# Logarithm and exponential from one activation table, the first stripe masked on VectorE by factor and triangle, stripe 1's products on the whole array, and another order of the written-out list

## The chip, the cores and the metric

The kernel runs on one core of a Trainium2 chip. The metric is the device time in microseconds (us). Before the change it is 226.11 us, the median of three runs (225.96 to 226.34). The profiled execution from which all durations below come took 225.86 us, of which 224.1 us are the span between its first and its last instruction.

## The reference

Two layers follow each other. The first is an attention without softmax whose weights decay with distance; it is written in blocks of 64 rows, with a state that is carried from block to block. The second is a two-layer perceptron on its output.

```python
# q, k, v: 4 batches x 8 heads x 768 rows x 64; lam: one number per head, 0.97 to 0.99
Dmask = np.where(rel >= 0, lam[:, None, None] ** rel[None, :, :], 0.0)
for b in range(nb):
    intra = np.einsum('bhic,bhjc->bhij', qb, kb) * Dmask[None]
    intra = np.einsum('bhij,bhjd->bhid', intra, vb)
    inter = np.einsum('bhid,bhde->bhie', qb * lam_pow[None], kv_state)
    out[:, :, sl] = intra + inter
    kv_state = lam_block * kv_state + np.einsum('bhsd,bhse->bhde', kb * rev_pow, vb)
...
h = x @ w_in                                  # 3072 x 512 by 512 x 2048
g = np.where(h >= 1, h, np.where(h <= -1, 0, (h + 1) ** 2 / 4))
return g @ w_out                              # 2048 x 512
```

## The kernel before

The 3072 rows are cut into eight stripes (`STRIPES`): stripe 0 has four blocks of 128 rows, stripe 1 two, the six others three each. Stripes 0 and 1 together are the first batch. A stripe's eight heads are worked in four pairs. The kernel works in blocks of 128 rows and not of 64, so the decay factors are taken for 128.

The decay is made once, at the start: `ln_lam` is the logarithm of `lam` (line 191, ScalarE), `ex` its product with positions (line 194, VectorE), `dec` the exponential (line 197, ScalarE). Logarithm and exponential come from two activation tables, and each is loaded by an ACT_TABLE_LOAD. `k` and `q` are multiplied by their factors while they are cast to bf16 (`att_cast`). The product of `k` and `q` then lacks one factor per head and the causal triangle: `mask`, built for a pair by two ScalarE instructions (`build_mask`, line 216), holds their product for each head, and one VectorE instruction per pair (`att_mask`, line 371) multiplies the scores by it.

What is done is not scheduled by a program. It is the string `ORDER`, a list of words in the order in which their instructions are recorded. Each engine, and each queue of transfers, executes its own part of the list in that order, and waits for what an instruction needs. A word has a letter, a stripe and a pair, and for casts an engine (a ScalarE, d VectorE, g GpSimd):

- `L01k` loads k of stripe 0, pair 1 (SyncE's queue); in stripes 1 to 3 one load covers two pairs, so `L10v` brings v of stripe 1 for the pairs 0 and 1. In stripe 0 a load of k or v is two transfers, one of q is a single one. `W0` to `W3` load quarters of `w_in`, `W4` to `W7` of `w_out`, on GpSimd's queue with a cast from f32 to bf16 (lines 232 and 236). `L10v@W2` means that this load waits until the one named has landed.
- `k`, `q`, `v` cast; `T`, `Q` transpose k and q on TensorE (line 334) and `t`, `u` copy the transposes out on ScalarE (lines 342, 344); `S` the scores (lines 358, 362), `s` the mask; `R` the new part of the state (lines 416, 422), `r` the state's update on VectorE (lines 435, 444); `O` the output of a pair (lines 472 to 504) and `o` its copy on ScalarE (lines 514, 516).
- `K` is `mlp_in_ko` (line 575): for stripe 0 alone, the part of the first three tiles of `x @ w_in` that needs one pair only. `P03` is one whole tile of `x @ w_in` (four products, line 561), `h03` its relu with bias (line 584, ScalarE), `A00` the rest of the activation for four tiles (lines 541 to 543, VectorE). `Y012` is a quarter of the second product for one block of 128 rows (line 593; the last digit is the quarter of `w_out`), `y` and `U` copy and store the result.
- `D1` and `D2` are one and two products of the identity with itself (line 549) that nobody reads. `B0a` builds a mask, `E` completes the factors of the scan in stripe 0, `J` clears the middle of the v and kz tiles, `G` clears zeros, `z` copies k into a tile with zeros beside it.

`FORMS` has a letter for each stripe, the form of its products. In form p the two heads of a pair use halves of the array: the products of `O` are 128x64 and 64x64 (lines 485 and 504), and the state of a pair is 128x64. In form f both heads use the whole array, with zeros beside the values: v and kz tiles have a zero middle, the state is 128x128 with zeros outside its two corners, the factor with the state is one product per block and not two (lines 472 and 493). In form w, from stripe 4, the transposes are made by DMA.

PSUM has four banks for the perceptron (`pmm`), two for transposes, states and outputs (`pat`), and one tile for the scores (`psp`), so the scores of a pair wait until the mask of the pair before has read them.

Of the kernel before, what the change touches and what calls it, by code (L numbers as in the profile page):

```python
# [8 lines left out]
F32 = mybir.dt.float32  # L9
# [33 lines left out]
v20g y02 T20 T21 Q20 h10 P19 t21 P18 k23d Y002 L21q@W5 v22d Y013 q22g z21a t20 u20 h18 R20 P11  # L43
S20 k22d y01 h19 Q21 P13 h11 P12 u21 L31k q23d P16 L30k z22a Y003 T22 h13 h12 U02 P17 P15 L31q
h16 t22 r20 s20 y00 h17 A10 S21 Q22 k32d s21 P1a u22 Q23 T23 h1a R21 r21 L30q u23 P14 L30v v23g
z23g P1c P1f h15 k33g q30g P1d h14 P1b q31g S22 h1f h1c L31v O20 L40k t23 R23 k31a A11 o20 h1d
s22 P1e Y100 R22 Y110 k30a r23 z31g v32g r22 Y111 S23 O21 h1b L40q h1e Q30 T30 A12 s23 o21 A13
L40v Y101 u30 t30 O22 z30g T31 z32a o22 Y112 O23 v31d G40 v30g Y102 Q31 o23 S30 P22 s30 G42 R31
v33g u31 q32d t31 h22 P23 R30 Y113 P21 r30 h23 R32 G41 P29 q33d z33a y11 h21 r31 T32 Q32 P20 r32
k40d t32 u32 R33 r33 P2b h29 S31 P27 O30 q40g U03 h20 s31 h2b o30 S32 q42g Y103 Q33 T33 s32 t33  # L50
O31 P25 G43 h27 L50k u33 o31 T40 P26 P24 h26 h24 O32 S33 A20 P2c v40d q41d s33 h25 h2c U01 y10
k42a P2a O33 P28 o32 h28 k43g v41g P2d P2f T42 A21 P2e o33 k41d h2a q43d h2d G50 h2e R40 P32 P31
h2f R41 S40 A22 r41 h32 v42a P30 T41 A23 s40 P33 h31 h30 h33 Y200 P34 Y201 P36 L50v P37 T43 Y202
Y203 k51a L50q U11 L60k h37 h36 y20 P35 v43a P3a h3a r40 S41 O40 h34 A30 s41 P39 o40 v51d h39
R42 k50a P3b r42 P38 O41 U10 S42 P3f h35 h38 o41 P3e s42 q50a h3f X40 h3e O42 P3c q52d o42 A31
R43 v50d P3d h3b S43 r43 T50 q51d h3c Y210 Y220 v52g Y211 h3d k52a s43 Y212 R51 A32 X41 L60q
Y300 Y320 O43 Y321 U00 A33 Y322 X42 Y213 o43 X43 S50 y21 Y221 T51 Y301 Y323 y32 Y302 Y303 T52
P41 P40 R52 s50 r51 S51 R50 y30 P42 L60v Y222 q60a k53a k61d Y223 q53a q62g r50 h42 q61g k60g
s51 T53 h41 P43 h43 h40 P4b S52 T60 r52 U21 Y310 P46 h46 Y311 h4b s52 O52 P44 k62g O50 v61g o52
A40 h44 v53d k63g q63g v62a O51 U20 P48 T62 P4d Y312 S53 y22 T61 o50 h4d h48 v60a o51 P4c P49  # L60
h4c P47 R60 U30 s53 S60 h49 h47 s60 Y313 X50 L70k R53 r60 P45 S61 h45 y31 P4f X52 L70q O60 v63a
o60 P4a P4e X51 h4f h4a r53 Y410 Y400 A41 O53 o53 q71g Y420 h4e A42 Y411 R61 A43 U32 Y421 Y401
Y412 Y402 R62 X53 s61 Y413 P57 k72a Y403 h57 T63 L70v k70g r61 r62 y41 P51 h51 P5a S62 s62 P50
O61 y40 v73d Y422 R63 P53 k73a h50 o61 h53 S63 h5a s63 k71g q70g P52 U40 v72d P58 Y423 T71 O62
h52 y42 P59 P54 h59 h54 T70 P56 h56 P5b r63 P55 O63 A50 S70 h55 o62 o63 q73d s70 P5d R73 P5f h58
r73 R72 U41 X61 U22 P5e h5d h5b h5f v70a h5e U31 X62 P5c Y500 X63 A51 X60 A52 Y510 R70 h5c Y501
S71 Y511 P60 P63 h63 Y512 h60 Y502 A53 P68 q72g T73 r72 s71 Y503 Y513 P62 h68 v71g h62 T72 P61
y51 h61 S72 P67 R71 P6a P65 h67 h6a s72 r70 P6b h6b P66 U51 O72 y50 P69 A60 S73 r71 P6f o72 s73
h66 P64 X72 O71 h6f h69 P6d Y520 o71 Y521 h6d O70 P6c A62 o70 X71 h64 O73 Y522 h65 h6c P6e Y523
Y610 Y600 A61 o73 h6e A63 y52 X70 Y611 Y612 U42 Y601 Y602 X73 P75 Y613 Y603 y61 P78 P70 y60 h78  # L70
h75 P76 h76 P7b h7b P73 Y620 P71 U50 h73 h70 P72 U52 P7a U61 h71 P79 Y621 h72 h7a h79 Y622 A72
Y623 P74 h74 y62 P77 P7e h77 h7e P7d P7f A70 P7c h7d h7f h7c U60 Y710 A71 Y700 Y711 Y701 Y712
U62 A73 Y713 Y702 Y703 y71 y70 U71 U70 Z72
"""


# [5 lines left out]
def kernel(  # L82
# [23 lines left out]
    NU = 1  # L106
    NZ = 3 if NU == 2 else 5
    NK = 3
    NKZ = 4 if "f" in FORMS else 0
    assert sum(c for _, _, c in STRIPES) * BLK == B * S  # L110

# [76 lines left out]
    nc.vector.memset(one, 1.0)  # L188

    ln_lam = const.tile([128, H], F32, name="ln_lam")  # L190
    nc.scalar.activation(out=ln_lam, in_=lam_b, func=AF.Ln)
    ex = const.tile([128, NR, H], F32, name="ex")
    pa, la = pos[:, :], ln_lam[:, :]
# [72 lines left out]
    st = {}  # L266

    def decay(row, h0, C, inner):

# [96 lines left out]
    def att_mask(u):  # L366

        s, hp = u
        C, T = shape(s)[:2]
        d = st[u]  # L370
        nc.vector.tensor_tensor(  # L371
            out=d["sc"][:, :, 0:C, :],
            in0=d["ps"][:, :, 0:T].rearrange("p h (c i) -> p h c i", c=C),
            in1=_ins(mask[:, 2 * hp:2 * hp + 2, :], 2, C), op=AX.mult)

    def before(u):

        s, hp = u
        C, T, first, last, fm = shape(s)
        if first:  # L380
            return None
        ss = st[s - 1, hp]["ss"]
        return ss[:, :, CM - 1] if s == 1 else ss[:, shape(s - 1)[0] - 1, :]

    def att_z(u, eng):
# [8 lines left out]
        else:  # L394
            (nc.gpsimd if eng == "g" else nc.vector).tensor_copy(dst, src)

    def att_r(u):

        s, hp = u
        C, T, first, last, fm = shape(s)  # L400
        d = st[u]
        n = C - 1 if last else C
        if fm != "p":
            d["pk"] = pk = pat.tile([128, CM, 2, D], F32, name="pk", tag="pat")
            d["ss"] = szp.tile([128, 3, 2 * D], BF16, name="sz", tag="sz")
        elif s == 0:
            d["pk"] = pk = pat.tile([128, D, CM], F32, name="pk", tag="pat")
# [43 lines left out]
    def att_o(u):  # L451
# [13 lines left out]
            d["xn"] = xn_pairs[s, hp // NU][:, hp % NU * T:hp % NU * T + T]  # L465
            d["po"] = po = pat.tile([128, CM, 2, D], F32, name="po", tag="pat")
        else:
            d["po"] = po = pat.tile([128, CM, 128], F32, name="po", tag="pat")
        for c in range(C):
            for hi in range(2):  # L470
                if fm == "f":
# [160 lines left out]
    for word in order(NS):  # L632
# [18 lines left out]
             "X": att_x}[f]((n[0], n[1]))  # L651
        elif f == "J":
            set_middles()
        elif f == "z":
            att_z((n[0], n[1]), word[3])
        elif f == "D":
# [49 lines left out]
```

## Time and profile before

| | us |
|---|---|
| median of three runs | 226.11 |
| the profiled execution | 225.86 |
| its span | 224.1 |
| TensorE busy | 214.2 |
| VectorE busy | 150.8 |
| ScalarE busy | 128.8 |
| GpSimd busy | 45.6 |

TensorE is busy 96% of the span. 868 of its 1683 products are those of lines 561 and 593, the perceptron. The share of busy time is not spread evenly: nearly all idle time of TensorE lies in the first 24 us, around 39 us, and behind 200 us.

The time of a single instruction is longer than its distance from the next of a kind, since TensorE's products overlap: a product with 512 columns is shown with 379 ns, while four of them follow each other in 0.86 us. For sums the chain of waits is used, which shows the distances.

### The profile page before, as it was taken

Reading aid. Unit: us, or ns where it says so; the run is one execution under the profiler, and the core shown is the slowest. Engines: PE = TensorE matmul, PEld = TensorE weight load, DVE = VectorE, ACT = ScalarE, POOL = GpSimd, SP = SyncE. Lnnn points to the kernel's source line nnn. Section 1 sums busy time; section 2 is a strip of 40 time slices with the busy share of each in tenths; the row PEclk is TensorE's granted clock in tenths of the full one; section 3 lists DMA queues with packets and bytes.
Section 4 is the critical chain, followed back from the end, with each engine's and each line's share of the span. In section 5 each row is a group of like instructions: output and inputs, shape, how many; then the busy total and the mean of one; then the engine's idle time right before and its main releaser. Section 6 shows DMA issues by size and latency. Waiting matters only on the chain.

```text
span 224.1 us, 4412 instructions
## 1 busy us (share of the span) xinstructions
PE 214.2 (96%) x1683; PEld 122.7 (55%) x1683; DVE 150.8 (67%) x236; ACT 128.8 (57%) x276; POOL 45.6 (20%) x90
## 2 busy tenths in 40 slices
PE   6498999999999999999999999999999999999994
PEld 1245544444776666656644666556665565455453
DVE  2547357885589888998894475993889486305930
ACT  5484277806886676958902766617682576074520
POOL 4453049002363442000102340061000000000000
PEclk9769999999999999999999999999999999999999
DMA  4999999998999992499899989899928104220112
GB/s 128 252 236 174 209 200 179 197 247 195 231 244 201 219 220 77 84 199 245 198 187 194 169 216 207 186 208 163 236 58 108 47 18 104 94 94 0 51 47 94
DMA packets 100629, 35.95 MB, mean 160 GB/s; under 512 B 89216, under 2 KB 97664, under 8 KB 100608
## 3 DMA queue, kind: packets, MB, share of 16 engines
q1 hardware_dynamic: 96384, 31.47, 65.6%
q0 software_dynamic: 4224, 4.19, 11.8%
q8 instruction: 13, 0.21, 0.4%
q14 instruction: 8, 0.07, 0.1%
HBM read 27.27 MB, written 6.29 MB: 150 GB/s over the span
## 4 chain that ended last, share of the span: by engine, by line
PE 87%; DVE 5%; DMA 2%; ACT 2%; SPq 2%; issue 1%; DVEq 0%; ACTq 0%
PE py L593 33%; PE ph L561 33%; PE pw L549 3%; PE pt L334 2%; PE ps L358 2%; DMA v_nat<-in_v_dram 2%; PE ps L362 2%; PE py L613 2%; PE pk L416 2%; DVE tt L542 1%; DVE gT L543 1%; PE po L472 1%; PE po L479 1%; PE ph L575 1%; SPq L162 1%; PE po L504 1%
## 5 line engine op out<-in xcount | busy, mean ns | idle before, releaser
L561 PE MATMUL ph<-xT,w_in_sb 128*128 128x384 bf16 (+2 forms) x500 | 90.9, 325 | 0.0
L584 ACT ACTIVATE tt<-ph,one 128x384 bf16<-128x384 f32 (+2 forms) x128 | 69.9, 592 | 32.5 <-PE ph L561 17.2
L593 PE MATMUL py<-w_out_sb,gT 128*128 128x512 bf16 x368 | 87.0, 379 | 0.3 <-DVE gT L543 0.3
L561 PEld LDWEIGHTS <-w_in_sb 128*128 128x128 bf16 x500 | 46.5, 98 | 28.8 <-issue 0.2
L593 PEld LDWEIGHTS <-gT 128*128 128x128 bf16 x368 | 34.5, 98 | 36.4 <-DVE gT L543 1.2
L371 DVE TENSOR_TENSOR sc<-ps,mask 128x768 bf16<-128x768 f32 (+2 forms) x32 | 30.5, 953 | 19.8 <-PE ps L358 14.2
L541 DVE TENSOR_SCALAR mm<-tt 128x1536 bf16<-128x1536 bf16 (+2 forms) x32 | 18.7, 583 | 21.8 <-ACT tt L584 20.8
L543 DVE TENSOR_TENSOR gT<-tt,mm 128x1536 bf16<-128x1536 bf16 (+2 forms) x32 | 31.7, 990 | 1.2
L542 DVE TENSOR_TENSOR tt<-tt,mm 128x1536 bf16<-128x1536 bf16 (+2 forms) x32 | 31.3, 979 | 1.1
L601 ACT COPY osb<-py 128x512 f32<-128x512 f32 x23 | 13.4, 584 | 23.3 <-PE py L593 23.3
L310 POOL TENSOR_TENSOR kq<-q_nat,dec 128x384 bf16<-128x384 f32 (+2 forms) x17 | 14.8, 890 | 48.4 <-DMA q_nat<-in_q_dram 35.6
L444 DVE SCALAR_TENSOR_TENSOR sz<-sz,lam_blk,pk 128x128 bf16<-128x128 bf16 x48 | 16.4, 346 | 1.7 <-PE pk L416 0.5
L287 POOL CAST vc<-v_nat 128x384 bf16<-128x384 f32 (+2 forms) x12 | 7.1, 588 | 48.1 <-PE po L498 31.5
L516 ACT CAST xT<-po 128x384 bf16<-128x384 f32 (+2 forms) x16 | 7.7, 481 | 15.3 <-PE po L504 11.7
L549 PE MATMUL pw<-ident 128*128 128x512 bf16 x31 | 11.5, 494 | 1.8 <-POOL ident masks.py:199 1.4
L334 PE MATMUL pt<-ident,kq 128*128 128x128 bf16 x96 | 9.8, 238 | 3.6 <-DVE kq L310 1.9
L310 DVE TENSOR_TENSOR kq<-k_nat,dec 128x384 bf16<-128x384 f32 (+2 forms) x11 | 7.5, 689 | 7.3 <-PE pk L416 4.6
L514 ACT CAST xn<-po 128x384 bf16<-128x384 f32 x16 | 7.7, 487 | 7.4 <-PE po L498 7.3
L334 PEld LDWEIGHTS <-kq 128*128 128x128 bf16 x96 | 7.1, 106 | 8.2 <-DVE kq L310 2.7
L301 ACT ACTIVATE kq<-k_nat,dec 128x192 bf16<-128x192 f32 (+2 forms) x26 | 10.6, 464 | 0.9 <-PE pk L416 0.9
L342 ACT COPY kqT<-pt 128x384 bf16<-128x384 bf16 (+2 forms) x16 | 7.7, 490 | 3.5 <-PE pt L334 3.5
L305 POOL TENSOR_SCALAR kq<-k_nat,dec 128x192 bf16<-128x192 f32 (+1 forms) x16 | 8.2, 528 | 2.9 <-PE pt L334 2.9
(74 smaller groups left out, 156.4 us busy)
## 6 DMA issues: line engine op xcount, KB each, us to landing
out_dram<-osb SPq DMA_DIRECT2D x23, 256.0 KB, 2.4
q_nat<-in_q_dram SPq DMA_DIRECT2D x18, 256.0 KB, 4.3
k_nat<-in_k_dram SPq DMA_DIRECT2D x24, 128.0 KB, 4.3
v_nat<-in_v_dram SPq DMA_DIRECT2D x24, 128.0 KB, 4.0
k_nat<-in_k_dram SPq DMA_DIRECT2D x12, 256.0 KB, 4.9
v_nat<-in_v_dram SPq DMA_DIRECT2D x12, 256.0 KB, 4.8
w_in_sb<-in_moe_w_in_dram POOLq DMA_DIRECT2D x4, 512.0 KB, 9.3
w_out_sb<-in_moe_w_out_dram POOLq DMA_DIRECT2D x4, 512.0 KB, 7.6
```

The costliest lines, as they stand in the source:

```text
L310: (nc.gpsimd if eng == "g" else nc.vector).tensor_tensor(dst, src, decay(row, 2 * hp, C, inner), op=AX.mult)
L334: nc.tensor.transpose(out=d["pt"][:, i, c, :], in_=d["kq"][:, i * C + c, :], identity=ident)
L371: nc.vector.tensor_tensor(out=d["sc"][:, :, 0:C, :], in0=d["ps"][:, :, 0:T].rearrange("p h (c i) -> p h c i", c=C), in1=_ins(mask[:, 2 * h ...
L444: nc.vector.scalar_tensor_tensor(out=d["ss"][:, c, :], in0=prev, scalar=lam_blk[:, hp:hp + 1], in1=kv, op0=AX.mult, op1=AX.add)
L541: nc.vector.tensor_scalar(mm, tt, 0.5, 1.0, AX.mult, AX.min)
L542: nc.vector.tensor_tensor(tt, tt, mm, op=AX.subtract)
L543: nc.vector.tensor_tensor(g[:, 4 * a:4 * a + 4, 0:T], tt, mm, op=AX.mult)
L549: nc.tensor.matmul(pw, lhsT=ident, rhs=_ins(ident[:, :], 1, 4), start=True, stop=True)
L561: nc.tensor.matmul(ph[:, 0:T], lhsT=w_in_sb[:, ko, ni * 128:(ni + 1) * 128], rhs=x_tiles[s][:, ko, 0:T], start=(ko == 0), stop=(ko == KO - 1))
L584: nc.scalar.activation(out=t_tiles[s, ni // 4][:, ni % 4, 0:T], in_=p_tiles[s, ni][:, 0:T], func=AF.Relu, bias=one[:, 0:1])
L593: nc.tensor.matmul(y_tiles[s, m], lhsT=g_tiles[s][:, ko, m * 128:(m + 1) * 128], rhs=w_out_sb[:, ko, :], start=(ko == 0), stop=(ko == FO - 1))
L601: nc.scalar.copy(out=osb, in_=y_tiles[s, m])
```

## The change

There are four parts.

1. The activation table that holds both logarithm and exponential is asked for ahead of line 191. In the built program there is one ACT_TABLE_LOAD and not two.
2. In stripe 0 the mask is not read. `att_mask` issues two VectorE instructions per pair, one for each head: scores times the head's factor (a column of `dec`) times the triangle `causal`. The masks are then needed from stripe 1 on, and their words stand elsewhere in the list.
3. `FORMS` is "pfffwwww": stripe 1 takes form f. It needs four `z` copies, the state of stripe 0 as 128x128 with zero corners (`corners`, cleared in `J` by four more GpSimd memsets, filled by the new words `b`: two copies of 64x64 per pair), and its state tiles are the wide ones.
4. The list is another one up to the word `P44`; the 309 words from there on are the same. Casts change engines, transfers and waits (`@`) stand elsewhere. There are as many `D1` (9) and `D2` (11) as before, at other places.

`bank`, `PK_PAT` and `PO_PAT` are new, but with all four entries 1 the tiles lie in the same pool as before.

```diff
-FORMS = "ppffwwww"
+FORMS = "pfffwwww"
 ORDER = """
-L00k D1 D1 L01q D2 D2 D1 L02q L01k q01d k00a k01d D1 T00 q02g L00q q00d L01v L02k D1 D2 T01 t00
-Q00 Q01 k02d v01a D1 B0a u00 S00 T02 D2 D1 B3a u01 L00v Q02 t01 L02v D2 E s00 S01 D2 L03q v02g
-v00a L03k u02 D2 W0 D1 R00 q03g B1a L03v W2 D2 D2 B2a s01 W1@L00v L11q t02 W3 R01 r00 S02 r01
-O00 v03g O01 o00 k03d D1 o01 T03 s02 L10v@W2 W4@L10v J Q03 t03 u03 R02 r02 S03 R03 O02 o02 D2
-r03 s03 K00 L10q@W1 K02 O03 W5@L02k q11g K01 q12d q10g o03 K03 h02 P03 L10k@W2 h01 P08 q13g L11k
-L11v k11g P0b h03 W6@L02q h00 P06 h08 h06 h0b P07 P04 P05 P09 W7@L00k h07 P0a Q12 h09 A00 Q10
-k13d L20k@W5 h05 P0f h0a h04 k12d P0d u10 k10a P0e v13g T10 t10 T12 t12 P0c L20q u12 S10 L21k@W6
-h0e D2 v10a h0f T11 T13 L20v Q13 A01 h0c Q11 Y030 u13 A02 s10 Y020 h0d t13 Y000 u11 Y010 t11
-Y011 R10 v12a v11a r10 R11 S11 Y031 Y021 s11 Y001 S12 r11 R13 q21g O10 o10 Y022 Y032 A03 r13 s12
-Y033 S13 R12 O11 Y012 y03 s13 r12 k20a o11 O13 k21a O12 q20d Y023 L21v@W1 o13 o12 z20a v21d P10
...
+L00q D2 E B2a D1 D2 D1 L02k q00d D2 B0a D2 L00k k00g L01v k02d T02 D2 T00 t00 Q00 L01k L02q k01a
+q02d u00 L00v L03q D2 Q02 T01 v00a L01q S00 s00 q01g t02 L03v q03d u02 L03k D2 D2 R00 r00 W0 D1
+L02v v01d Q01 W1 t01 u01 v03d D2 D2 k03g W2@L00v Q03 S01 O00 v02g D2 L10q u03 T03 o00 D1 L11q
+R01 L10v@W1 s01 S02 r01 s02 O01 B1a t03 R02 o01 r02 S03 R03 O02 r03 K01 q10g K00 s03 o02 O03 o03
+K02 Q10 P03 L10k L11k q11d h03 Q11 K03 h00 P07 h01 P06 h02 h06 P05 W3@L01v J W4@L10v P0b P09
+L11v u10 v11g k11g h07 A00 W5@L01k q12d P0a B3a h05 L20k@W5 h0b P08 k12g W6@L01v q13d h09 u11
+k10a P0e h0e k13d z11g T10 P04 t10 T11 P0c h04 S10 t11 h08 P0d Q13 v10d W7@L03k L21k@W6 h0c T13
+Q12 s10 z10d S11 t13 D1 P0f u13 b10a R10 L20q b11g T12 z12a h0a v12g Y010 t12 A01 h0d Y020 L20v
+b13g h0f Y000 Y030 L21q@W6 r10 O10 v13a k20a Y031 A02 Y001 o10 Y021 b12g Y002 Y022 A03 Y011 k23g
+Y023 Y003 R11 u12 s11 R12 Y012 S12 k22d z13d r12 R13 z20g Y032 s12 y02 r13 z22a S13 s13 r11 D1
+O12 k21g q20d L30q o12 y00 Y033 v20d O13 O11 Y013 o11 L21v Q20 T20 o13 P10 v21g q21d y03 P11 Q21
...
     ln_lam = const.tile([128, H], F32, name="ln_lam")
+    nc.scalar.preload_act_table_set("natural_log_exp_and_others")
     nc.scalar.activation(out=ln_lam, in_=lam_b, func=AF.Ln)
...
+    corners = [const.tile([128, 128], BF16, name=f"bd{i}") for i in range(NP if FORMS[1] == "f" else 0)]
...
     def set_middles():
         for t in vc_all + kz_all:
             nc.gpsimd.memset(t[:, :, 1, :], 0.0)
+        for t in corners:
+            nc.gpsimd.memset(t, 0.0)
...
         d = st[u]
+        if s == 0 and STT:
+            for hi in range(2):
+                nc.vector.scalar_tensor_tensor(
+                    out=d["sc"][:, hi, 0:C, :],
+                    in0=d["ps"][:, hi, 0:T].rearrange("p (c i) -> p c i", c=C),
+                    scalar=dec[:, 2, 2 * hp + hi:2 * hp + hi + 1],
+                    in1=_ins(causal[:, :], 1, C), op0=AX.mult, op1=AX.mult)
+            return
         nc.vector.tensor_tensor(
...
+        if fm == "f" and FORMS[s - 1] == "p":
+            return corners[hp]
...
+    def att_b(u, eng):
+
+        s, hp = u
+        ss = st[s - 1, hp]["ss"]
+        last = ss[:, :, CM - 1] if s == 1 else ss[:, shape(s - 1)[0] - 1, :]
+        for hi in range(2):
+            p0 = hi * D
+            o = corners[hp][p0:p0 + D, p0:p0 + D]
+            if eng == "a":
+                nc.scalar.copy(out=o, in_=last[p0:p0 + D])
+            else:
+                (nc.gpsimd if eng == "g" else nc.vector).tensor_copy(o, last[p0:p0 + D])
...
```

More of the change, by code (lines that the diff above doesn't have):

```diff
@@ L43 @@
[L43 to L72, printed above, removed]
@@ new lines @@
+t20 u20 P17 R20 S20 h11 L30k q22g y01 P1b P13 r20 T21 s20 L31k h17 P12 z21d h10 h13 L31q u21 P16
+q23d P1a q31g v23g O20 h12 U02 P14 t21 L30v T22 h1b Q22 P15 o20 k31g L31v h16 t22 u22 S21 D1 Q23
+z23d P18 A10 h15 s21 h14 R21 h1a T23 P1c P19 t23 r21 v22g P1e A11 L40k S22 h1c u23 T31 P1f h18
+h19 k30a O21 P1d Q31 t31 o21 Y100 s22 Y101 u31 q30d S23 h1e R22 T30 Y110 A12 h1f L40q t30 s23
+Q30 Y102 v30g u30 R23 k32a r22 q33g S30 r23 D1 z30g O22 Y111 o22 R30 h1d A13 O23 Y112 q32g s30
+o23 z31a z32a P20 T32 G42 v32g v31d k33d h20 P2b Q32 t32 h2b Y103 S31 u32 G40 G41 r30 D1 Y113
@@ new lines @@
+y11 U03 L50k R31 P23 P22 h23 L40v h22 s31 R32 P21 v33g h21 r31 G43 z33g T33 S32 Q33 k42d q42a
+P25 t33 r32 P29 s32 A20 h25 P27 R33 y10 u33 P26 h26 P2a k41a O30 h27 P24 h2a S33 q40a L50q P28
+q41g r33 h24 U10 P2c o30 k40d h29 h28 O31 P2e k43d o31 s33 h2c P2d P2f q43a h2f A21 v41g G50
+v43a O32 T40 o32 O33 o33 T41 Y200 h2d A22 Y201 h2e P33 P3a R41 R43 P31 A23 h3a v42a q50g k50g
+h31 P32 r41 h32 r43 Y202 P30 Y203 h33 S40 R42 P37 h30 P39 s40 r42 A30 q52a h39 T43 U00 P36 S41
+h37 h36 P35 P34 s41 P38 T42 T50 y20 h34 Y210 h35 P3d A31 h38 h3d L50v S42 P3f v40g P3c P3b h3f
@@ new lines @@
+r72 s71 Y503 Y513 P62 h68 v71g h62 T72 P61 y51 h61 S72 P67 R71 P6a P65 h67 h6a s72 r70 P6b h6b
+P66 U51 O72 y50 P69 A60 S73 r71 P6f o72 s73 h66 P64 X72 O71 h6f h69 P6d Y520 o71 Y521 h6d O70
+P6c A62 o70 X71 h64 O73 Y522 h65 h6c P6e Y523 Y610 Y600 A61 o73 h6e A63 y52 X70 Y611 Y612 U42
+Y601 Y602 X73 P75 Y613 Y603 y61 P78 P70 y60 h78 h75 P76 h76 P7b h7b P73 Y620 P71 U50 h73 h70 P72
+U52 P7a U61 h71 P79 Y621 h72 h7a h79 Y622 A72 Y623 P74 h74 y62 P77 P7e h77 h7e P7d P7f A70 P7c
+h7d h7f h7c U60 Y710 A71 Y700 Y711 Y701 Y712 U62 A73 Y713 Y702 Y703 y71 y70 U71 U70 Z72
@@ L108 @@
     NK = 3
+    STT = True
+    PK_PAT, PO_PAT = (1, 1, 1, 1), (1, 1, 1, 1)
     NKZ = 4 if "f" in FORMS else 0
@@ L266, with bank @@
     st = {}
+    def bank(pool, name):
+        n = CM * (D if name == "pk" else BLK)
+        return pool.tile([128, 512], F32, name=name, tag="pat" if pool is pat else "pmm")[:, 0:n]
     def decay(row, h0, C, inner):
@@ L406, in att_r @@
         elif s == 0:
-            d["pk"] = pk = pat.tile([128, D, CM], F32, name="pk", tag="pat")
+            d["pk"] = pk = bank(pat if PK_PAT[hp] else pmm, "pk").rearrange("p (e c) -> p e c", c=CM)
             d["ss"] = ssp.tile([128, D, CM], BF16, name="ss", tag="ss")
@@ L467, in att_o @@
         else:
-            d["po"] = po = pat.tile([128, CM, 128], F32, name="po", tag="pat")
+            d["po"] = po = bank(pmm if s == 0 and not PO_PAT[hp] else pat, "po").rearrange(
+                "p (c i) -> p c i", c=CM)
         for c in range(C):
@@ L653 @@
             set_middles()
+        elif f == "b":
+            att_b((n[0], n[1]), word[3])
         elif f == "z":
```

13 lines of the change are left out of this document (12 added, 1 removed).

## The prediction

> **What bounds the kernel now.** I read the page's busy times first, then short windows, then the chain of waits, then the queues of ScalarE and GpSimd. The page says that TensorE has work nearly always:
>
> ```profile
> PE 214.2 (96%) x1683; PEld 122.7 (55%) x1683; DVE 150.8 (67%) x236; ACT 128.8 (57%) x276; POOL 45.6 (20%) x90
> ```
>
> So only 9.9 us of the span are idle on TensorE, and what it does needlessly counts as busy. The windows show where both lie (columns: stretch, its length, busy time and count of PE, PEld, DVE, ACT, POOL, then granted clock, DMA share, GB/s):
>
> ```profile
> 4.00:8.00 4.00, 2.07 (x10) 0.55 (x8) 1.29 (x4) 3.05 (x5) 0.82 (x1) 1.00 0.99 279
> 8.00:12.00 4.00, 2.23 (x17) 1.49 (x19) 2.52 (x3) 1.90 (x6) 1.52 (x2) 0.57 1.14 228
> 12.00:16.00 4.00, 4.00 (x30) 1.95 (x27) 1.24 (x3) 3.12 (x9) 2.51 (x3) 0.57 1.14 248
> 16.00:20.00 4.00, 4.00 (x57) 2.10 (x55) 3.14 (x5) 1.20 (x4) 2.93 (x5) 1.00 1.13 167
> 20.00:24.00 4.00, 3.18 (x60) 2.32 (x57) 2.75 (x5) 2.36 (x5) 0.00 (x0) 1.00 1.19 197
> 36.00:44.00 8.00, 7.59 (x48) 3.72 (x46) 6.75 (x7) 7.14 (x19) 3.28 (x6) 1.00 1.22 201
> ```
>
> From 8 to about 15.4 us the clock is half. TensorE's idle time lies before 24 us, a last 0.4 us around 39, and then little until the tail, whose list doesn't change. The chain of waits (start, length, what) tells when useful dense work begins:
>
> ```profile
> 19.05 0.34 PE po L485 x8
> 19.39 0.32 PE po L504 x6
> ...
> 23.61 0.54 PE pw L549 x2
> 24.15 1.29 PE ph L575 x6
> 25.44 0.34 PE po L485 x8
> ...
> 27.60 7.84 PE ph L561 x36
> ...
> 39.49 0.60 ACT tt L584
> 40.13 0.59 PE pw L549 x2
> ...
> 41.17 4.32 PE py L593 x20
> ...
> 73.50 0.34 PE po L472 x6
> ```
>
> At 24.15 the first `K` starts, at 27.60 all twelve of its products are done, and TensorE then runs at its rate. So the end is moved by four things alone: when that point is reached, which fillers (`pw`, unread) stand behind it, how many products there are, and new stalls.
>
> **The change part by part.** *One table.* The second load is behind the logarithm:
>
> ```profile
> 0.80 1.28 ACT L191 ACT_TABLE_LOAD   x1 [0.80 <-PEq L690]
> 3.99 1.28 ACT L197 ACT_TABLE_LOAD   x1
> ```
>
> Without it the exponential waits for `ex` (done at 4.27) and not until 5.28, so the factors come 1.0 us earlier. The first load stays, hidden ahead of the logarithm's own wait until 3.76. The 1.0 us is no term: it serves casts whose loads land at 5 us and later; without that cover it would be worth 1.0.
>
> *Loads and first products.* SyncE issues the loads in slots; the k-th transfer goes out when the k-th went out before (10th at 6.69, 14th near 9.1), and lands 3.9 us later for k and v, 4.2 for q (medians of the first 20 us). `L02q` is now 10th: 10.9, cast 0.69 to 0.91, ready 11.7. TensorE until then: ten fillers to 5.9 (eight took 3.59), `T02` 7.4, a filler, `T00` 8.9, `Q00`, a filler. Then `Q02`, `T01` and `S00`, to 13.1 at half clock. `L01q` is 14th: 13.3, GpSimd's cast 1.06, 14.4. Behind it on GpSimd stand W0 and W1 (0.96 and 0.78), then `k03g`, W2, `v02g`: `T03` gets its k at about 17.4. W0 goes out at 14.4 against 14.03 before. The tile's view gives the time to landing, and GpSimd's timeline the later quarters:
>
> ```profile
> DMA to landing us min/median/max: 7.2/9.3/12.4
> ```
>
> ```profile
> 30.97 0.74 POOL L236 DMA_DIRECT2D w_out_sb<-in_moe_w_out_dram  x1 [12.04 <-DMA v_nat<-in_v_dram]
> 33.51 0.76 POOL L236 DMA_DIRECT2D w_out_sb<-in_moe_w_out_dram  x1
> 34.27 1.99 POOL L310 TENSOR_TENSOR kq<-q_nat,dec 128x256 bf16<-128x256 f32 x3
> 36.92 1.91 POOL L236 DMA_DIRECT2D w_out_sb<-in_moe_w_out_dram  x2
> ```
>
> The first quarter is the one of 7.2 us, so W0 lands at 21.6, or 22.6 if the second q load of stripe 1, now ahead of it, costs its 256 KB at 248 GB/s (1.06).
>
> *The masks.* One product of scores and mask for a pair took 1.22 us (128x1024); each of the two that replace it covers 128x512. Such a width took 0.69 with a mask; by the two widths of the state's update (0.274 at 64, 0.346 at 128, so 1.1 ns a column) the new form would take 0.78. So 1.38 to 1.56 a pair, 0.16 to 0.34 more, on VectorE. In return eight ScalarE masks of 0.39 are no longer due before the first scores. VectorE is then the path: behind `S01` follow s01, r01 (scan, 0.69), s02, r02, since the scores' tile is single and `S02` waits for s01, `S03` for s02. With half clock until 15.4, as before, the fillers and `R00`, `Q01`, `Q03` put `S01` at 17.3 to 17.6; then 1.5, 0.7, 1.4, 0.7 give 22 and the last products of `O02` 22.6. `K01` would start at 22.7, `O03` would follow s03 (25.0), `P03` its copy (25.7), and the point that before was reached at 28.46 (twelve `K` products and `P03`) at 27.2: 1.2 us earlier. With full clock from 12.0 everything is 1 us earlier, bounded by W0: 2.2. I take 1.5, nearer to the clock that the trace shows: **-1.5** (bounds -1.2 and -2.2).
>
> By the Trainium skill, "TensorE: Matmul & The Clock Gate", Part 1: The HAM clock gate, the clock is halved after an idle window of some 3.4 us, restored after a busy one, and the windows run free of the kernel's start; the trace's one half-clock stretch of about two such lengths agrees. By that rule either bound above can come out.
>
> *Fillers.* Before, the last two stand at 40.13, behind that point, all others ahead. Now five single ones stand behind it. A product of 512 columns costs 0.216 there (4.32 for 20): three more are **+0.65** (0 if all fall into waits).
>
> *Stripe 1's form.* For a pair the old `O` is four half-array products at 0.34/8 and four at 0.32/6: 0.38. The new one is six at 0.34/6 (line 472): 0.34. Four pairs: **-0.2** (bounds -0.4, where eight products vanish at 53 ns, and 0). The Trainium skill, "TensorEngine Tiling (Array Packing)", Overview, promises up to twofold speed where a dimension is 64 or less, which speaks against giving up the halves. By it the four products would cost 0.34 and not 0.17 a pair, and the sum of four pairs would be about +0.3; the rows show 43 against 57 ns, a third and not twofold.
>
> Its copies: four `z` and four `b` pairs, 0.2 to 0.5 each, on three engines, four memsets of 0.2 in `J`, state updates 0.346 instead of 0.274. All run under the 13.8 us of stripe 0's `P` words (64 at 0.216); without that cover `b` and `r` would cost some 1 us.
>
> *The wait around 39.* Stripe 1's transposes stood behind the last `P`, so TensorE waited for copies: 0.41 idle. Now `T10`, `T11` and `S10` have `P` words between them: **-0.4** (bounds -0.4 and +0.3). Later casts move between engines where windows have TensorE full; cost 0, covered by `P1` to `P3`, bounds 0 and the third rival's price.
>
> Sum: -1.5 + 0.65 - 0.2 - 0.4 = -1.45, so 224.4 against the profiled 225.86. The median of the runs is 0.25 above that profile: **224.7 us**. All terms at their ends at once would give 223.1 and 225.9 there; with few of them at an end, its own range is 223.6 to 225.6.
>
> **The rivals.** *First: w_out holds what was gained.* W4 waits for `L10v`, this for the second quarter of `w_in`, as before, so it may not land before 38.5 (30.97 + 7.5). The first `Y` needs it: 41.17 less 1.5, less the wait and fillers there (0.8), plus one filler and `R10` (0.4) is 39.3. The margin is 0.8; with one more q load (1.06) and 0.4 of later issue ahead, 0.6 of stall, and with W5 to W7 likewise late up to 1.2: 225.9. Against it: W6 and W7 no longer stand behind three q casts, and can go out at 34 to 36 and not at 36.92 and 38.08. 0.16.
>
> *Second, slower: the clock stays half through a third stretch.* 8 to 12 us has TensorE busy 2.23 of 4, and after it the clock was half; now it does about as much there. If also 12 to 15.4 fails, 15.4 to 18.8 runs at half and does 1.7 us less work: the lead of 1.2 becomes a loss of 0.5, and 0.5 + 0.65 - 0.2 - 0.4 gives 226.4, 226.7 as a median. It decides from more than 1.5 us of TensorE idle between 12 and 15.4. Against it: the list has enough fillers there. 0.07.
>
> *Third, slower: GpSimd's queue in stripes 2 and 3.* Stripe 2 gives it k of the pairs 1 and 3 (two of 0.55 each) and one more v (0.59) for one q (0.91), and stripe 3 three q and one k for two q and one k: some 2.8 us more. `k23g`, `z20g` and `k21g` stand in a row (2.8 us) ahead of `T21`. `L21k` waits for W6 (out near 34.5, some 7.7 to land, then three issues of 0.55 and 3.9: near 48 to 50); the turn of `T21` comes near 54 (39.3 and 16 `Y` words of 0.86, with some smaller work). If these loads land over 1.2 us later, each pair's transposes wait some 0.6 us, over four pairs 2.4: 227.1. For it: a q cast of 384 columns took 0.84 on a quiet GpSimd and 1.21 beside VectorE. Against: GpSimd is busy only 12.7 of 30 us from 50 to 80 (3.47, 4.83 and 4.42 in windows of ten). 0.14.
>
> **How the numbers follow.** The forecast has 0.63. Less than 0.2% (0.45 us) can't be told from no change here. Faster: the forecast nearly whole, and a quarter of the first rival, 0.66; same: 0.13, the rest of the first and the forecast's edge; slower: the second and third, 0.21. The range is 223.5 to 226.7: it holds the forecast's bounds, the first rival and the second, and leaves out most of the third.
>
> **What would show it.** Right: one ACT_TABLE_LOAD; the first `K` product near 22 to 23; the first `py` at 39 to 40 with no wait for w_out before it; TensorE full from there. Wrong: granted clock 0.5 beyond 15.4; idle TensorE before `T21` with GpSimd named; `py` waiting for landings at 42 to 48.

## The result, and the profile after

The changed kernel takes 224.13 us, the median of four runs (223.85 to 224.44), against 226.09 us (225.96 to 226.34) for the kernel before on the same chip. The ratio is 0.991, with a 95% interval of 0.989 to 0.993. The forecast was 224.7. The profiled execution took 224.41 us with a span of 222.7, against 225.86 and 224.1: 1.45 us less. Here and below, medians and ranges leave out four executions in a slower state (227.10 and 446.56 us of e6_more_fillers, 328.53 of h2_rest, 228.64 of e11_f_early_zeros).

The page of the changed kernel begins with busy times, in the same order as before:

```profile
PE 214.3 (96%) x1675; PEld 123.2 (55%) x1675; DVE 151.1 (68%) x240; ACT 127.6 (57%) x275; POOL 56.7 (25%) x112
```

TensorE is as busy as before (214.2), so the span fell by idle time alone: 222.7 - 214.3 is 8.4 where 9.9 us stood. The busy time stayed although eight products are gone: the 31 fillers, at other places now, are busy 12.4 us and not 11.5. The windows show where the idle time went (stretch, its length, busy time and count of PE, PEld, DVE, ACT, POOL, then clock, DMA share, GB/s):

```profile
8.00:12.00 4.00, 2.78 (x20) 1.56 (x22) 0.69 (x1) 2.45 (x5) 0.00 (x0) 0.60 1.07 274
12.00:16.00 4.00, 4.00 (x28) 1.85 (x28) 3.27 (x5) 1.25 (x4) 2.57 (x3) 0.55 1.24 236
36.00:44.00 8.00, 8.00 (x56) 3.96 (x55) 7.06 (x9) 5.46 (x14) 5.64 (x10) 1.00 1.12 171
```

The granted clock is half in much the same stretch as before, 8.8 to 15.6 us. From 36 to 44 us TensorE no longer waits at all. The chain of waits (start, length, what) gives the points that the forecast was about:

```profile
22.82 1.40 PE ph L609 x6
...
27.53 7.07 PE ph L595 x32
...
39.64 3.45 PE py L627 x16
```

The first `K` is at 22.82 (24.15 before), the twelve `K` products and `P03` are done at 27.53 (28.46), the first `Y` is at 39.64 (41.17). The one table load that is left, by the timeline of ScalarE, and the two mask instructions of a pair, by the timeline of VectorE:

```profile
0.80 1.28 ACT L193 ACT_TABLE_LOAD   x1 [0.80 <-PEq L726]
```

```profile
17.45 1.41 DVE L383 SCALAR_TENSOR_TENSOR sc<-ps,dec,causal 128x512 bf16<-128x512 f32 x2 [0.73 <-PE ps L372]
```

A pair of them takes 1.41 us, where 1.38 to 1.56 was estimated. The quarters of `w_in` land 6.5 to 10.0 us after their issue (7.2 to 12.4 before), and GpSimd's timeline gives two of the four issues of `w_out`:

```profile
30.55 0.74 POOL L239 DMA_DIRECT2D w_out_sb<-in_moe_w_out_dram  x1 [7.94 <-PE ph L595]
...
36.45 0.74 POOL L239 DMA_DIRECT2D w_out_sb<-in_moe_w_out_dram  x1
```

W0 goes out at 14.42 and lands 6.5 us later, at 21.0. W4 goes out at 30.55, no later than before, and the last quarter 1.6 us earlier than before (38.08): the `Y` words never wait for `w_out`.

### The profile page after: what moved, and what is told of

Same layout as the page of the kernel before. It is cut to its first block, busy times and chain, and to the rows that moved or that the text cites. A ratio compares the mean times of both kernels' runs of the same rounds, so it can differ in the third digit from the quotient of the medians.

```text
span 222.7 us, 4420 instructions
## 1 busy us (share of the span) xinstructions
PE 214.3 (96%) x1675; PEld 123.2 (55%) x1675; DVE 151.1 (68%) x240; ACT 127.6 (57%) x275; POOL 56.7 (25%) x112
## 4 chain that ended last, share of the span: by engine, by line
PE 83%; DVE 10%; SPq 2%; DMA 2%; issue 1%; ACT 1%; DVEq 0%
PE py L627 33%; PE ph L595 32%; PE ps L368 2%; DVE gT L577 2%; DVE tt L576 2%; PE pw L583 2%; SPq L164 2%; DMA q_nat<-in_q_dram 2%; PE pt L344 2%; PE py L647 2%; PE pk L449 2%; DVE mm L575 2%; PE ps L372 1%; PE po L506 1%; PE ph L609 1%; PE po L513 1%
## 5 line engine op out<-in xcount | busy, mean ns | idle before, releaser
L618 ACT ACTIVATE tt<-ph,one 128x384 bf16<-128x384 f32 (+2 forms) x128 | 70.7, 587 | 32.6 <-PE ph L595 21.6
L389 DVE TENSOR_TENSOR sc<-ps,mask 128x768 bf16<-128x768 f32 (+1 forms) x28 | 25.6, 916 | 18.4 <-PE ps L368 14.4
L575 DVE TENSOR_SCALAR mm<-tt 128x1536 bf16<-128x1536 bf16 (+2 forms) x32 | 20.8, 649 | 20.7 <-ACT tt L618 19.5
L315 POOL TENSOR_SCALAR kq<-k_nat,dec 128x192 bf16<-128x192 f32 (+2 forms) x28 | 15.1, 550 | 31.1 <-PE pk L449 11.7
L320 POOL TENSOR_TENSOR kq<-q_nat,dec 128x384 bf16<-128x384 f32 (+2 forms) x14 | 13.7, 983 | 25.8 <-DMA q_nat<-in_q_dram 25.5
L297 POOL CAST vc<-v_nat 128x384 bf16<-128x384 f32 (+2 forms) x14 | 8.5, 609 | 30.7 <-PE po L532 10.6
L583 PE MATMUL pw<-ident 128*128 128x512 bf16 x31 | 12.4, 513 | 1.4 <-POOL ident masks.py:199 1.4
L344 PE MATMUL pt<-ident,kq 128*128 128x128 bf16 x96 | 10.6, 233 | 2.6 <-DVE kq L320 2.0
L311 ACT ACTIVATE kq<-k_nat,dec 128x192 bf16<-128x192 f32 (+2 forms) x20 | 8.2, 456 | 7.0 <-DMA k_nat<-in_k_dram 6.1
L320 DVE TENSOR_TENSOR kq<-q_nat,dec 128x384 bf16<-128x384 f32 (+2 forms) x12 | 7.6, 643 | 3.2 <-DMA q_nat<-in_q_dram 3.2
```

What stands on the lines that cost most here:

```text
L315: nc.gpsimd.tensor_scalar(dst[:, hi, :, :], src[:, hi, :, :], dec[:, row, 2 * hp + hi:2 * hp + hi + 1], 0.0, AX.mult, AX.add)
L320: (nc.gpsimd if eng == "g" else nc.vector).tensor_tensor(dst, src, decay(row, 2 * hp, C, inner), op=AX.mult)
L344: nc.tensor.transpose(out=d["pt"][:, i, c, :], in_=d["kq"][:, i * C + c, :], identity=ident)
L389: nc.vector.tensor_tensor(out=d["sc"][:, :, 0:C, :], in0=d["ps"][:, :, 0:T].rearrange("p h (c i) -> p h c i", c=C), in1=_ins(mask[:, 2 * h ...
L575: nc.vector.tensor_scalar(mm, tt, 0.5, 1.0, AX.mult, AX.min)
L583: nc.tensor.matmul(pw, lhsT=ident, rhs=_ins(ident[:, :], 1, 4), start=True, stop=True)
```

## The experiments

"Ratio" is to the kernel before on the same chip, whose median was 226.1 to 226.2 throughout. "The changed kernel" is 224.13 with ratio 0.991.

| kernel | median us (lowest to highest) | ratio, 95% interval |
|---|---|---|
| e1_two_tables | 224.13 (223.43 to 224.46) | 0.990 (0.988 to 0.993) |
| e2_mask_tile | 223.89 (223.49 to 224.32) | 0.989 (0.987 to 0.992) |
| e3_no_late_fillers | 223.23 (222.52 to 223.42) | 0.986 (0.984 to 0.988) |
| e4_form_p | 225.49 (224.88 to 227.56) | 0.998 (0.996 to 1.000) |
| e6_more_fillers | 223.74 (222.70 to 224.08) | 0.989 (0.986 to 0.991) |
| h1_head | 224.48 (223.38 to 226.05) | 0.992 (0.990 to 0.995) |
| h2_rest | 236.74 (236.12 to 236.99) | 1.046 (1.044 to 1.048) |
| e7_form_f_alone | 226.31 (225.65 to 226.74) | 1.001 (0.999 to 1.002) |
| e11_f_early_zeros | 225.10 (224.40 to 226.42) | 0.996 (0.994 to 0.998) |
| e9_half_before | 237.41 (236.47 to 238.42) | 1.049 (1.047 to 1.052) |
| e10_full_before | 226.86 (225.98 to 228.05) | 1.003 (1.001 to 1.005) |
| e8_best | 223.46 (222.50 to 224.40) | 0.987 (0.985 to 0.990) |

### The table and the masks

e1_two_tables, the changed kernel without the table asked for:

```diff
-    nc.scalar.preload_act_table_set("natural_log_exp_and_others")
```

> The changed kernel with the request for the common table taken out, so that logarithm and exponential load a table each again. Theory (the 1.0 us by which the factors come earlier is hidden behind the loads): 0 to 0.3 us slower than the changed kernel, 224.1 to 224.4; the first product of K stays at 22.8. Rival (the factors are on the path: in the changed kernel's trace the first cast starts at 5.16, right behind them, while its load had landed at 4.7): K at 23.8 and 1.0 us more, 225.1.

The time is the changed kernel's to the hundredth. VectorE's first cast begins at 6.14 us and not at 5.16, but the cast of `Q02`, which waits for its load, begins at 10.24 in both: the table's 1.0 us is hidden behind the loads.

e2_mask_tile, the changed kernel with the prepared mask in stripe 0, the words for the masks of pairs 1 and 3 moved forward so that all four are there in time:

```diff
-    STT = True
+    STT = False
-L00q D2 E B2a D1 D2 D1 L02k q00d D2 B0a D2 ...
+L00q D2 E B2a D1 D2 D1 L02k q00d D2 B0a B1a B3a D2 ...
```

> The changed kernel, but stripe 0 is masked from the mask tile again, one VectorE instruction per pair; the masks of the pairs 1 and 3 are built right behind those of 2 and 0, where ScalarE is idle from 6.1 to 8.4. Theory (VectorE's s01, r01, s02, r02 set when K starts): two masks on that path at 1.22 and not 1.41 (two halves, as the changed kernel's trace shows) bring K 0.4 us earlier and the end 0.3 to 0.4, 223.8. Rival (the masks on ScalarE delay the first transposes' copies, or K waits for something else): 0 or slower.

0.24 us less than the changed kernel, and inside its spread. In the profile the products that lead up to the first `K` end at 22.73, and at 22.82 in the changed kernel, so the shorter masks bring `K` forward by 0.1 and not by the 0.4 expected. Factor and triangle on VectorE gain nothing: the eight ScalarE instructions of the mask fit in early as well. What brought `K` forward is the order of the list, not the new mask.

### The fillers

e3_no_late_fillers, the five single `D1` behind `K01` taken out:

```diff
-... Q12 s10 z10d S11 t13 D1 P0f u13 ...
+... Q12 s10 z10d S11 t13 P0f u13 ...
```

> The changed kernel without the five single unread products that stand behind the first product of K. Theory (TensorE's stream sets the end, so each costs its 0.216): 1.1 us less, 223.0. Rival A (they stand in waits that the profile doesn't show because the filler hides them): 0 to 0.3 less. Rival B (they keep the clock up): slower, with granted clock 0.5 somewhere behind 24 us.

0.90 us less, 0.18 for each product, where 0.216 would be all of it. In the profiled execution the clock was full and the first `K` came some 0.9 us earlier as well, and yet its span is only 1.1 us shorter. The rest comes back as waiting, as the window of this profile shows; the changed kernel has TensorE full there:

```profile
60.00:70.00 10.00, 9.10 (x105) 6.36 (x103) 9.72 (x16) 8.44 (x23) 4.26 (x6) 1.00 0.91 218
```

VectorE is busy 9.72 of these 10 us, in the changed kernel too, and there the chain of waits runs through VectorE from 57.86 to 70.7 us, through state updates, masks, casts and the activation:

```profile
57.86 0.30 DVE sz L475
...
69.99 0.70 DVE gT L577
```

In e3's profile VectorE's instructions follow each other without a wait from 57.6 to 72 us. The last part of an activation there (`gT`) begins 1.3 us earlier than in the changed kernel at first (60.86 against 62.19), and 0.7 earlier at the end (69.25 against 69.99): lead is lost on the way. The changed kernel just meets this bound: TensorE is idle 0.14 us from 60 to 80. A greater lead is passed on only in part.

e6_more_fillers has ten more filler products ahead of `T02`, `Q00` and `Q02`, where TensorE still waited:

```diff
-... k02d T02 D2 T00 t00 Q00 ... L03q D2 Q02 ...
+... k02d D2 D2 D1 T02 D2 T00 t00 D2 D1 Q00 ... L03q D2 D2 Q02 ...
```

> The changed kernel with ten more unread products ahead of the first transposes and in TensorE's early waits, 41 in all. Theory (the half clock from 8.8 to 15.6 costs the lead 0.9 us, as in the profile of the run without late fillers, where it was full and K began at 21.8): granted clock 1.0 from 5 us on in the profile and in most executions, K at 21.8 to 22.0, 0.3 to 0.9 less than the changed kernel. Rival (the clock falls anyway, and the products delay the transposes): half clock as before and K at 23 or later, 0 to 0.5 more.

The four executions that count have a mean granted clock of 0.998 or 1.0, where three of the changed kernel's four have 0.985: the early fillers seem to keep the clock up, as expected. There is no profile of one of them. The 0.4 us by which the median is lower is at the low end of what was expected and cannot be told from the changed kernel (intervals 0.986 to 0.991 and 0.989 to 0.993). So early fillers cost nothing, and what they bring is small; late ones cost nearly their whole length.

### Form f on the new list

e4_form_p, the changed kernel with stripe 1 in form p, without the words that fill the tiles of form f:

```diff
-FORMS = "pfffwwww"
+FORMS = "ppffwwww"
```

> The changed kernel with stripe 1 in form p again: no zero-padded copies of its k, no corners, eight products more, halves of the array. Theory (products alone count, copies are hidden): 0.2 us slower than the changed kernel (0 to 0.4), 224.3. Rival (the copies hold transposes and state updates up): 0.3 to 1.0 faster, 223.1 to 223.8.

1.36 us more than the changed kernel, where the forecast had 0.2 for the form. The profiled execution took 227.56, for a reason given below, so its times are not compared with the changed kernel's from the start, but the same stretch of words can be. The chain of waits of the changed kernel, then of e4_form_p, for the output of one pair and the `Y` word behind it:

```profile
53.10 0.22 PE po L506 x4
53.32 0.11 PE po L527 x2
53.43 0.86 PE py L627 x4
```

```profile
55.82 0.23 PE po L519 x4
56.05 0.26 PE po L538 x4
56.31 0.97 PE py L627 x4
```

Two things differ. The output takes 0.49 and not 0.33 us. And the same four full-array products behind it take 0.97 and not 0.86, though nothing in them changed. From the `R` word ahead of the first `Y` to the transposes behind the last of these groups the chain has 16.36 us in the changed kernel (39.47 to 55.83) and 17.76 in e4_form_p (41.47 to 59.23). Of the 1.40, four outputs make 0.62, whole-array products that stand right behind products of half the array some 0.65 (five `Y` groups and two transposes, 0.11 each time), and the `R` words 0.15. That accounts for the 1.36 us between the medians.

The long time of that execution has another cause, in the same chain:

```profile
14.47 8.83 DMA w_in_sb<-in_moe_w_in_dram
...
23.65 2.34 PE ph L609 x5
```

W0 took 8.83 us to land (6.5 in the changed kernel), and the five `K` products ran into a stretch of half clock. The forecast had named this bound on an earlier `K`, not its spread.

### The price of a change between the whole array and half of it

Two kernels measure the 0.11 us by itself. Ahead of each of the 48 groups of `w_in` in stripes 4 to 6, where TensorE is busy throughout (80.00 of 80 us from 110 to 190), stands one more product that the group overwrites:

```diff
         p_tiles[s, ni] = ph = pmm.tile([128, 512], F32, name="ph", tag="pmm")
+        if s in (4, 5, 6):
+            nc.tensor.matmul(ph[:, 0:128], lhsT=ident[0:64, :], rhs=ident[0:64, :],
+                             start=True, stop=True)
```

e10_full_before has `ident[0:128, :]` in both places.

> The changed kernel with one more product ahead of each of the 48 groups of w_in in stripes 4, 5 and 6 (its result is overwritten by the group): 64 rows by 128 columns of the identity against 128 columns, that is half of the array. TensorE is busy throughout there, so all of its time shows. Theory (a full-array product behind a half-array product costs 0.11 us more than behind another full-array one, as the groups of 0.97 against 0.86 us suggest): 48 x (0.055 + 0.11) = 7.9 us more than the changed kernel, about 232.0, and 5.3 us more than e10_full_before. Rival (no price of a change; the groups of 0.97 us waited for something else): 48 x 0.055 = 2.6 us more, about 226.8, as e10_full_before.

> The same as e9_half_before with the extra product on the whole array: 128 rows by 128 columns of the identity against 128 columns. Both theories: 48 x 0.055 = 2.6 us more than the changed kernel, about 226.8. If it comes out at e9's time, the array's halves cost nothing by themselves.

The whole-array product costs 226.86 - 224.13 = 2.73 us, 0.057 each, as both theories had it. The half-array product, with the same 128 columns and half of the rows, costs 237.41 - 226.86 = 10.55 us more, 0.22 each: twice what was expected. The timelines of TensorE say why, first e9_half_before, then e10_full_before, two extra products and the group between them:

```profile
127.07 0.23 PE L595 MATMUL ph<-ident 64*128 64x128 bf16 x1
127.23 0.82 PE L598 MATMUL ph<-xT,w_in_sb 128*128 128x384 bf16 x4
127.98 0.23 PE L595 MATMUL ph<-ident 64*128 64x128 bf16 x1
```

```profile
126.26 0.22 PE L595 MATMUL ph<-ident 128*128 128x128 bf16 x1
126.31 0.81 PE L598 MATMUL ph<-xT,w_in_sb 128*128 128x384 bf16 x4
126.96 0.22 PE L595 MATMUL ph<-ident 128*128 128x128 bf16 x1
```

The first column is the start. From the extra product to the group it is 0.16 us for the half and 0.05 for the whole array; from the group to the next extra product 0.75 against 0.65. So both ways cost: some 0.11 us out of the half array, from the extra product to the group, and 0.10 into it, from the group to the next extra product. The 96 changes make 10.55 us, 0.11 each. The Trainium skill, "TensorEngine Tiling (Array Packing)", Key Properties, says that changing the tiling mode drains the engine. These runs agree in so far as a change costs 0.11 us, more than the product itself; whether the engine drains for it they do not show.

With that the output of form p can be read. The timeline of the kernel before has one of stripe 1's outputs and the start of the next:

```profile
53.66 0.30 PE L485 MATMUL po<-sc,vc 128*64 128x128 bf16 x4
53.89 0.27 PE L504 MATMUL po<-kqT,ss 64*64 64x128 bf16 x2
54.00 0.22 PE L504 MATMUL po<-kqT,sr 64*64 64x128 bf16 x2
54.15 0.30 PE L485 MATMUL po<-sc,vc 128*64 128x128 bf16 x4
```

It is 0.49 us long, and no whole-array product stands in it. The trace's single starts show that the products of the two heads start together, 0.003 us apart, and that two such pairs of one form follow each other in 0.08 or 0.11 us (0.053 where more of them stand in a row, as in stripe 0), but a pair of one form and the first of another in 0.15. Four pairs at 0.053 would be 0.21 us; the other 0.28 goes with the two changes, from 128x64 to 64x64 and back. So a change from one half-array form to another costs some 0.1 us as well, and by this reckoning form p would be the shorter one without them (form f takes 0.33 for its six whole-array products). No run measures that by itself.

### Form f on the old list

e7_form_f_alone keeps the old list, the prepared mask and two tables, and adds only the words that form f needs:

```diff
-FORMS = "ppffwwww"
+FORMS = "pfffwwww"
-... L11v k11g P0b ... W7@L00k h07 P0a ... v13g T10 ...
+... L11v k11g P0b ... W7@L00k z11g h07 P0a ... v13g b11g b13g b12g T10 ...
```

> The kernel before with stripe 1 in form f alone: the four copies of k and the four pairs of corners put into the old list, behind W7, behind v13 and between VectorE's masks of stripe 1; everything else as before. Theory (a product on half the array costs the next full one 0.11 us, so that form p costs 0.3 to 0.4 per pair): 1.2 to 1.5 less than before, 224.7. Rival A (only the eight products count): 0.2 to 0.4 less, 225.8. Rival B (the copies hold up the transposes): slower than before.

No gain. In its windows TensorE is idle 1.42 us from 33 to 36 and 0.92 from 39 to 42, where the kernel before has none and 0.40. GpSimd's timeline shows what is late:

```profile
33.25 0.67 POOL L265 MEMSET bd<- 128x128 bf16 x4
...
36.58 2.10 POOL L314 TENSOR_SCALAR kq<-k_nat,dec 128x128 bf16<-128x128 f32 x2
```

The new clearing in `J` stands behind W4, which had waited for a load until 30.71, and ahead of stripe 1's q and k. The q casts come 0.3 us later than before. TensorE, which in this execution had its first `K` at 23.1 and so was some 0.9 us ahead of the kernel before, waits 1.4 us for them: its lead is lost here. And two k casts that took 0.72 in the kernel before, with nothing on VectorE, took 2.10 beside VectorE's long instructions.

e11_f_early_zeros puts `J` and one corner ahead of W4, where GpSimd waited 11 us anyway, and `z11g` and the other corners behind stripe 1's v cast:

```diff
-... T03 s02 L10v@W2 W4@L10v J Q03 ... W7@L00k z11g ... v13g b11g b13g b12g ...
+... T03 s02 J b11g L10v@W2 W4@L10v Q03 ... W7@L00k ... v13g z11g b13g b12g ...
```

> Form f alone in the old list again (e7_form_f_alone, 226.3), with GpSimd's zeroing of the padded tiles and one corner copy put ahead of W4's issue, where GpSimd waited 11 us anyway, and the other copies behind stripe 1's v cast, so that W5, W6 and the q casts of stripe 1 come no later than in the kernel before. Theory (form f is worth about 1.4 us, and in e7 its own GpSimd work gave that back as 1.4 us of waiting at 34 to 36 and 0.9 us at 40): about 224.8, between 224.3 and 225.3. Rival (form f is worth the 0.2 us of the prediction in the old list, and more only beside the new one): 226.0.

225.10: the same products as e7, 1.2 us less, and some 1 us less than the kernel before (0.9 by the ratio, 0.5 to 1.4 by its interval). GpSimd's timeline now has

```profile
20.80 0.68 POOL L265 MEMSET bd<- 128x128 bf16 x4
...
34.34 0.72 POOL L314 TENSOR_SCALAR kq<-k_nat,dec 128x128 bf16<-128x128 f32 x2
```

and TensorE's 1.4 us of waiting before 36 us are gone; the 0.9 around 40 stay. So form f is worth about 1 us on the old list if its GpSimd work lies where GpSimd has nothing to do, and nothing if it lies ahead of stripe 1's casts.

### Head and rest of the list

h1_head has the new list up to `K02`, the new masks and one table, stripe 1 in form p, and behind `K02` the words that are left in the old order. h2_rest is the reverse: the old list up to `K03`, then the rest in the new order with form f.

```diff
-FORMS = "pfffwwww"
+FORMS = "ppffwwww"
-... r03 K01 q10g K00 s03 o02 O03 o03 K02 Q10 P03 L10k ...   (new order)
+... r03 K01 q10g K00 s03 o02 O03 o03 K02 ...                (old order)
```

> The new list up to K02 with one table and the two VectorE masks per pair, and behind it the words of the old list that are then left, stripe 1 in form p, one pair of unread products behind K as before. Theory (the head's lead carries over to the end): the first product of K near 22.8 and not 24.0, so 0.9 to 1.2 us less than before, 225.0. Rival (what bounds the old list behind K, the quarters of w_out or the copies around 39, takes the lead back): the first product of Y at 41.0 as before, and 225.9 to 226.2.

> The old list up to K03 with two tables and the mask tile, and behind it the words of the new list that are then left, stripe 1 in form f, five single unread products behind K (34 in all). Theory (the rest's own gain, without the lead): form f 1.4 less, by the run with form p, three unread products more at 0.22: 225.3 to 225.5. Rival (the gains come only with the lead): 226 or more.

h1: 224.48, 1.7 us less than the kernel before, by the head alone, with two filler products behind `K01` and not five. That is more than the 0.9 to 1.2 expected. Its profile is of an execution of 226.05, in which W0 landed only at 23.34, so it does not tell where the rest comes from. h2 does not measure what it was meant to: the new rest transposes stripe 1's q right behind `K03`, and in the old head GpSimd casts it behind W4, which goes out at 30.86. TensorE waits 8.4 us for that cast, until 36.02, and the clock is half from 32 to 42. It shows only that the new rest needs the new head's early cast of stripe 1's q.

### The parts that paid, together

e8_best is e2_mask_tile and e3_no_late_fillers in one.

```diff
-    STT = True
+    STT = False
-L00q D2 E B2a D1 D2 D1 L02k q00d D2 B0a D2 ...
+L00q D2 E B2a D1 D2 D1 L02k q00d D2 B0a B1a B3a D2 ...
-... Q12 s10 z10d S11 t13 D1 P0f u13 ...
+... Q12 s10 z10d S11 t13 P0f u13 ...
```

> The changed kernel with three things that earlier runs favoured put together: masks of stripe 0 from one prepared tile (built early, as in e2_mask_tile), and none of the five dummy groups behind K01 (as in e3_no_late_fillers). Theory (every late dummy group is TensorE time that nothing hides, so the two gains add): e3 came to 223.2 against 224.1 and e2 to 223.9, so 223.0, between 222.6 and 223.4. Rival (the dummies keep the granted clock up, and e3's profile had full clock by luck of its phase): the half-clock stretch comes back later, and the run ends at 224.0 or above.

223.46, no better than e3_no_late_fillers (223.23), so the two do not add; the mask's 0.24 was spread. Three of its six executions have a mean granted clock of 0.985, as three of e3's have, so a stretch of half clock comes in some of them with or without late fillers; where it lies is not known, since the profile is of an execution with full clock. The interval of e3 (0.984 to 0.988) lies below the changed kernel's (0.989 to 0.993); that of e8 (0.985 to 0.990) overlaps it.

## Why the prediction was right, point by point

The direction and the sum held: -1.45 was forecast on the profile, and -1.45 was measured. The sum was right because two of its terms were off by half a microsecond in opposite directions; that it agrees to the hundredth is luck.

- **TensorE's work sets the end: right for this lead.** Idle time fell by 1.5 us, and what TensorE did needlessly (late fillers, changes between halves and whole) showed in the time nearly in full in e3, e9 and e10. The forecast did not see that VectorE takes the chain over from 57.86 to 70.74 us; it costs 0.14 us here and more in e3.
- **One table, no term: right.** e1 takes it away and loses nothing.
- **Loads and first products: right within 0.7 us, all a little early.** `Q02`'s cast, forecast to begin at 10.9, began at 10.24; `S01`, forecast for 17.3 to 17.6, began at 17.01; W0 landed at 21.0, forecast 21.6 to 22.6.
- **Start of dense work, -1.5: too much.** The first `K` came at 22.82 (22.7 forecast), but its twelve products and `P03` were done 0.93 us earlier than before, outside the term's bounds. The half clock had been the case to take (27.2 forecast for it, 27.53 measured); I leaned towards the full clock, which this execution did not have. The chain shows what makes the other 0.33: two words of transposes of stripe 1 (0.22) that I left out, and a change from the output's half array to `K` (0.10). In the profile of e8 the clock was full from 8 us on, `K` began at 22.08, behind W0 that landed at 21.8, and the twelve products and `P03` were done at 26.50, 1.96 us earlier than before: near the bound of 2.2 us.
- **The masks' place in that term: wrong cause.** The two instructions cost what was estimated, but e2 keeps the old mask and loses nothing. The lead is the order's.
- **Fillers, +0.65: right.** e3's 0.18 a product makes 0.54 for three.
- **Form f, -0.2: too little, and the term that was most mis-sized.** I took the old output at 0.38 us a pair from stripe 0, where eight products of a form stand together. In stripe 1 it takes 0.47 to 0.49 by the single starts, against 0.34 after: 0.6 for the four. The changes around the scores and outputs and the `R` words, which I left out, make 0.1 more. So it is -0.7 from one list to the other; in e11, on the old list, -0.7 by the same count and -0.9 by the time; and 1.36 on the new list, where form p's words would stand singly among whole-array groups. The 0.97 us groups were in the trace of before. The sentence on the Trainium skill there weighed twofold speed for halves against 43 and 57 ns. The 43 ns contain the changes: between them the halves do run two at a time (0.053 us a pair), and it is the changes that take this back. (At that rate the old output would be 0.21 us a pair and the term +0.5, not the +0.3 given there.)
- **Its copies hidden: right as placed,** with the price of the lost cover shown by e7: 1.2 us between e7 and e11, forecast some 1.
- **The wait around 39, -0.4: right.** 8.00 of 8 us from 36 to 44, 7.59 before.
- **w_out holds the gain: did not happen.** W4 went out at 30.55 and not after 30.97, and the last quarter 1.6 us sooner.
- **Half clock through a third stretch: did not happen** in this kernel's profile; the stretch ended at 15.64. That it can come is seen in e4's profile, from 23.5 to 26.9.
- **GpSimd's queue in stripes 2 and 3: did not happen.** GpSimd is busy 8.1 of 20 us from 60 to 80, and TensorE is idle 0.14 there, behind VectorE.

With the measured sizes the terms make -0.93 + 0.54 - 0.7 - 0.41 = -1.5, and with the 0.14 of waiting behind VectorE -1.36, against -1.45 in the profile. The medians differ by 1.96. That is more than the profiled pair shows, and so is h1's 1.7 for the head alone; the lead of 1.96 us in e8's profile, at full clock, is a likely cause, but the changed kernel's own execution at full clock (223.85) has an equal at 0.985, so this stays open.

## What to carry to other kernels

Price a product by rows with the same neighbours: a product on part of the array between whole-array groups costs two changes more than its own length, and a change between two kinds of part costs too. So either stand products of one form together or give them the whole array with zeros. Fillers that keep the clock up are free only where the engine would wait; behind the point from which it is full, each costs its length. A lead is worth its full length only up to the next bound, here VectorE at 58 to 71 us. And when clearing or copying is added to a queue, put it where that queue waits for a load, not behind the wait.

## What the runs showed of the hardware

- A change between products on the whole array and on 64 rows costs TensorE about 0.11 us each way (10.55 us for 96 changes), with the same columns.
- Products on two halves of the array run at the same time: in the trace of the kernel before the two heads' products start 0.003 us apart, and pairs of one form 0.053 us apart in a row, against 0.056 for single whole-array products of 128 columns. From one half-array form to another (64x128, 128x64, 64x64) it is 0.15.
- Two casts of k on GpSimd, 128x128 each, take three times as long beside VectorE. The changed kernel's profile has both: 2.14 us at 31.66, with VectorE busy for 2.14 of them, and 0.72 at 34.64, with VectorE idle. The kernel before has 0.72 with VectorE idle, e7 2.10 beside long VectorE instructions.
- The first quarter of `w_in`, issued at 14.0 to 15.2 us, landed 6.2 to 8.8 us later from one profiled execution to another. In e4, h1 and e10 this set the first `K` (23.5 to 23.7).
- A stretch of half clock was there in some executions of a kernel and not in others: the changed kernel's four have a mean granted clock of 1.0 once, at 223.85 us, and of 0.985 three times, at 223.85 to 224.44. The profiles put it between 8 and 16 us in the kernel before, the changed kernel, e1, e2, e9 and e10, and at 23.5 to 26.9 in e4.
